# Banded attention and a feed-forward layer in one kernel: the order of its work planned anew, output rooms and the read of a flag moved

## The chip, the cores and the metric

The kernel runs on one core of one Trainium2 chip. The metric is the device time of one execution in microseconds (us); for several runs it is their median. The engines of the core are TensorE (PE, with its weight loads as PEld), VectorE (DVE), ScalarE (ACT), GpSimd (POOL) and SyncE (SP), which here only issues DMAs. Each takes its own instructions strictly in order.

## What is computed

Attention over a band of 96 keys and 8 global keys with a distance bias, for 4 batches of 8 heads, 768 positions and 64 channels, and then a feed-forward layer with a leaky step on the 3072 x 512 result:

```python
scores = scale * np.matmul(q, k.transpose(0, 1, 3, 2))
...
bias = -slopes[:, None, None] * dist[None, :, :]
scores = np.where(keep, scores + bias[None, :, :, :], -1000000000.0)
a = np.exp(scores - np.max(scores, axis=-1, keepdims=True))
a = a / (np.sum(a, axis=-1, keepdims=True) + 1e-09)
x = np.matmul(a, v)          # then to (3072, 512)
...
h = x @ w_in                 # (512, 2048)
g = np.maximum(0.01 * h, h)
return (g @ w_out).astype(np.float32)
```

## The kernel before

All of the fast path is one list of words, `ORDER`, written out in the file by a planner. `fast_path` reads it word by word, and each word issues a few instructions, pinned to that order on their engines. A word is a letter for the kind of work, a number for the unit or turn, and perhaps a part. An engine runs its own instructions in the order in which their words stand, and waits where data or a room is not ready; so what stands ahead of an instruction on its own engine can hold it up.

**Attention** has 48 units of 4 heads x 128 queries. Lq, Lk, Lv load the operands (SP). S makes the scores (PE, into `ps_av`), B adds the bias and takes the maximum (DVE, in four parts .0 to .3, L333), E the exponential (ACT, L349), N the reciprocal of the sum and M the quotients (DVE). From unit 16 on D turns 32 x 32 blocks (DVE, L391) and writes the result to memory (SP, L360), and I fetches it back in four DMAs (SP, L366): I must wait in SP's queue until the write has landed. V multiplies with the values (PE, L470) into the free columns of a `ps_av` tile that also holds the scores of a later unit; Xh copies the result out (ACT, L480).

**The feed-forward layer** starts with chunks 0 to 2 of the rows, in words F (first product, PE), g (gates, on ACT and DVE in turns), H (second product, PE) and P (outputs). The weights come as 64-bit floats in pieces: Lw loads one (SP, L227), c converts it in four parts on ACT and DVE. The rooms of `load_piece` are four. Each product is made of three: the operands are split into a high part, rounded to a shorter format, and the rest. O stores the converted second weights to memory (SP, L708), R brings them back (POOL's DMA queue, L711).

**Chunks 3 to 6** take two blocks of weight columns at a time, in turns Q, y, d, r, h, l, J. A group of 8 turns serves one chunk of 512 rows: turns 0 to 7, 8 to 15, 16 to 23, 24 to 31. The first product is made in seven half-size products Q p.1 to Q p.7 of combined weights and operands instead of eight. C (16 parts: 12 passes on POOL, L664, and 4 roundings on ACT, L667) builds the combined weights of a turn once, during the turns before; A (POOL, L717), Y (ACT) and z (POOL or DVE) combine the operands of a chunk. The y word copies the first product out of its PSUM tile (ACT, L731), and Q p.2, which writes the same columns, waits for it. The words d add up the seven products (DVE, L737), r is the leaky step (DVE, L741), h the rounding (ACT, L744), l the rest (DVE, L747). J p.ij are the second products (PE, L755), issued a turn later among the Q of turn p + 1. At a chunk's end U copies four accumulators out (`late`; ACT L763, or DVE L761 with a `v`) and sends each to the output (SP, L765): U3 to U6, each with parts 0 to 3. The room `ob` of a part is `at((14, 20)[tt % 2], [DM])`: two rooms in turns. So parts 2 and 3 wait until the DMAs of parts 0 and 1 have landed.

**The flag.** The fast path is right for short bands only. Behind it `band_holds` tests the counts and the maxima (small DVE passes, L885 to L891), turns the column of 128 results with a product (PE, L894), reduces it (L895), casts it (L896), and `values_load` brings it into a register of each engine (L1086). A branch on it (L1088) skips a general path behind it, and the program's end follows (L1142).

**Planner's leads before.** From unit 16 on S of a unit n + 2 stands with V of unit n, in the same `ps_av` tile (`bank(n + 2)`).

Of the kernel before, what the change touches and what calls it, by code (L numbers as in the profile page):

```python
# [11 lines left out]
F32 = mybir.dt.float32  # L12
# [7 lines left out]
P = 128  # L20
# [38 lines left out]
P22.1 Lv17 P22.2 Xh14 Xl14 T15 g24a S16 g24b K15 k15 H23 Lk19 B16.0 g24c B16.1 E16.0 B16.2 B16.3 E16.1 g24d E16.2 V15
E16.3 N16 F25 M16.0 Lv18 Xh15 M16.1 M16.2 Xl15 M16.3 D16 S17 g25a H24 g25b I16 B17.0 g25c B17.1 E17.0 B17.2 Lq10 B17.3  # L60
E17.1 g25d F26 E17.2 Lk20 E17.3 N17 M17.0 M17.1 M17.2 V16 M17.3 g26a D17 S18 Lv19 Xh16 g26b H25 B18.0 g26c B18.1 E18.0
B18.2 I17 B18.3 E18.1 g26d E18.2 F27 Lk21 E18.3 N18 M18.0 M18.1 M18.2 M18.3 H26 D18 g27a g27b g27c I18 V17 g27d S19
Xh17 Lv20 F28 Lq11 B19.0 B19.1 E19.0 B19.2 Lk22 B19.3 E19.1 E19.2 E19.3 H27 g28a N19 M19.0 M19.1 M19.2 M19.3 D19 F29
g28b g28c I19 g28d V18 g29a g29b S20 Lv21 Xh18 Y3.0 H28 Lk23 B20.0 g29c B20.1 B20.2 E20.0 B20.3 E20.1 g29d E20.2 z3.0
F30 E20.3 N20 M20.0 M20.1 M20.2 M20.3 H29 D20 g30a g30b g30c V19 I20 g30d S21 Xh19 Lv22 F31 Lq12 B21.0 B21.1 E21.0
B21.2 Lk24 B21.3 E21.1 E21.2 E21.3 H30 g31a N21 M21.0 M21.1 M21.2 M21.3 D21 F32 g31b V20 g31c I21 g32a g31d S22 Xh20
g32b Lv23 H31 B22.0 B22.1 Lk25 E22.0 B22.2 B22.3 E22.1 E22.2 E22.3 F33 P31.0 g32c g32d P31.1 V21 g33a P31.2 H32 Xh21
g33b Lv24 N22 g33c M22.0 F34 M22.1 g33d M22.2 M22.3 D22 H33 g34a g34b F35 g34c I22 g34d H34 g35a g35b g35c F36 g35d
H35 g36a g36b g36c F37 g36d H36 g37a g37b g37c S23 g37d F38 Lq13 B23.0 B23.1 E23.0 B23.2 Lk26 B23.3 E23.1 H37 E23.2
g38a E23.3 g38b F39 N23 g38c C0.0 M23.0 g38d C0.1 M23.1 H38 M23.2 g39a M23.3 C0.2 D23 C0.4 C0.3 F40 g39b C0.5 g39c I23  # L70
g39d C0.6 V22 g40a C0.8 C0.7 g40b S24 Lv25 Xh22 C0.10 H39 g40c Lk27 B24.0 B24.1 C0.9 g40d A3.1 E24.0 B24.2 E24.1 B24.3
F41 E24.2 C0.11 E24.3 Y3.4 N24 C0.12 H40 M24.0 g41a M24.1 M24.2 C0.14 g41b C0.13 M24.3 g41c F42 D24 C0.15 C1.0 g41d
V23 z3.4 C1.1 g42a I24 g42b H41 C1.2 Xh23 g42c A3.2 Lv26 C1.3 g42d S25 F43 Lq14 B25.0 A3.3 Y3.5 B25.1 B25.2 Lk28 B25.3
E25.0 z3.5 E25.1 H42 A3.4 g43a E25.2 g43b E25.3 F44 C1.4 g43c N25 Y3.1 g43d C1.5 M25.0 Y3.6 M25.1 H43 M25.2 C1.6 M25.3
g44a D25 C1.8 C1.7 V24 g44b C1.10 C1.9 S26 g44c C1.11 I25 Xh24 F45 g44d B26.0 C1.12 B26.1 E26.0 Lv27 B26.2 C1.14 B26.3
E26.1 H44 Lk29 g45a z3.1p E26.2 g45b E26.3 F46 g45c N26 C1.13 z3.6p g45d M26.0 H45 M26.1 g46a M26.2 M26.3 C1.15 g46b
D26 g46c F47 C2.0 g46d C2.1 H46 C2.2 g47a I26 Y3.2 g47b C2.4 C2.3 z3.2 Q0.1 g47c C2.8 Y3.3 Q0.6 g47d C2.5 y0.1 z3.3
H47 C2.9 C2.6 d0a C2.11 C2.7 Q0.2 P47.0 C2.10 Q0.5 d0b C2.12 V25 d0c Q0.3 C2.14 C2.13 Lv28 Xh25 S27 C2.15 d0d r0.0
# [24 lines left out]
d9a E35.3 J8.01 d9b Q9.5 N35 M35.0 M35.1 J8.02 M35.2 d9c Q9.3 M35.3 D35 J8.03 d9d Q9.7 R10.0 r9.0 J8.10 I35 d9e h9.0
J8.11 d9f l9.0 Q9.4 J8.12 d9g J8.13 r9.1 V34 h9.1 R10.1 S36 l9.1 Lv37 Xh34 Q10.1 B36.0 B36.1 E36.0 J9.00 B36.2 B36.3
y10.1 Q10.6 E36.1 Lk39 E36.2 Q10.2 E36.3 d10a N36 J9.01 d10b Q10.5 M36.0 M36.1 M36.2 M36.3 J9.02 D36 Q10.3 d10c J9.03
d10d Q10.7 r10.0 I36 R11.0 J9.10 h10.0 d10e J9.11 d10f l10.0 Q10.4 J9.12 d10g J9.13 r10.1 V35 h10.1 R11.1 S37 l10.1
Lv38 Xh35 Q11.1 Lq20 B37.0 B37.1 E37.0 J10.00 B37.2 Lk40 B37.3 y11.1 Q11.6 E37.1 E37.2 Q11.2 E37.3 d11a N37 J10.01
d11b Q11.5 M37.0 M37.1 M37.2 M37.3 J10.02 D37 Q11.3 d11c J10.03 d11d Q11.7 r11.0 I37 R12.0 J10.10 h11.0 d11e J10.11
# [53 lines left out]
def fast_path(ctx, tc, qp, kp, vp, wi, wo, nvec, weights, woboth, nmall, out, B, H, S):  # L162
# [380 lines left out]
    def step(word):  # L543
# [602 lines left out]
```

## Time and profile before

| | us |
|---|---|
| median of 3 runs | 682.49 (681.49 to 683.00) |
| the profiled execution | 680.44 |
| its span, first to last instruction | 678.6 |
| outside its span | 1.84 |
| mean granted clock of TensorE | 0.978 |
| PE busy | 629.2 (93%) |
| DVE busy | 486.6 (72%) |
| ACT busy | 279.8 (41%) |
| POOL busy | 204.3 (30%) |

The busy shares are means over stages that differ: which engine others wait for is read from the stretch. A window's granted clock is a mean too: 1.00 is 2.4 GHz throughout, 0.50 is 1.2 GHz throughout.

### The profile page before, as it was taken

How to read it: one execution, taken by the hardware profiler on the slowest of the kernel's cores; microseconds unless marked ns; L12 is line 12 of the kernel's file. 1: busy time of each engine (PE TensorE's matmuls, PEld its weight loads, DVE VectorE, ACT ScalarE, POOL GpSimd, SP SyncE). 2: the span in 40 equal slices, each digit the busy share in tenths (PEclk: the TensorE clock that was granted, in tenths of full speed). 3: DMA queues.
4: the chain of work that ended last, by engine and by line, in shares of the span. 5: the costliest groups of instructions: out<-in, count | busy, mean ns of one | idle time of the engine just before them, and what ended most of it. 6: DMA issues, size and time to landing. Idle time of an engine off the chain costs nothing. (4 is left out here: it accounts for less than half of the span.)

```text
span 678.6 us, 16087 instructions
## 1 busy us (share of the span) xinstructions
PE 629.2 (93%) x6187; PEld 540.9 (80%) x6187; DVE 486.6 (72%) x1277; ACT 279.8 (41%) x802; POOL 204.3 (30%) x267
## 2 busy tenths in 40 slices
PE   5599999999999998889899799999989999999993
PEld 4478888898888867778688688888778888989982
DVE  6899998875666597988578566778757767555551
ACT  4877766546453455524225232324332223211111
POOL 3433401004100289887636001116100115211100
PEclk9879999999999999999899989999989999999998
DMA  8766744696666233446485865665775653533421
GB/s 282 255 202 193 224 136 141 213 397 209 189 182 211 82 115 125 136 128 188 142 248 150 240 195 171 205 194 177 206 224 164 197 145 88 160 94 94 125 63 68
DMA packets 71334, 118.07 MB, mean 174 GB/s; under 512 B 8784, under 2 KB 27216, under 8 KB 71248
## 3 DMA queue, kind: packets, MB, share of 16 engines
q1 hardware_dynamic: 54928, 85.48, 39.3%
q0 software_dynamic: 16320, 31.46, 16.6%
q8 instruction: 51, 0.84, 0.5%
q14 instruction: 35, 0.29, 0.1%
HBM read 90.18 MB, written 26.74 MB: 172 GB/s over the span
## 5 line engine op out<-in xcount | busy, mean ns | idle before, releaser
L744 ACT CAST rounded<-room 128x512 fp32r<-128x512 f32 x64 | 39.7, 620 | 199.2 <-DVE room L741 155.2
L711 POOL DMA_DIRECT2D wo<-w x60 | 43.5, 726 | 234.5 <-PE ps_two L755 232.3
L755 PE MATMUL ps_o<-wo,rounded 128*128 128x512 f32 x320 | 96.6, 400 | 0.0
L755 PE MATMUL ps_two<-wo,rounded 128*128 128x512 f32 x320 | 95.5, 396 | 0.0
L349 ACT ACTIVATE pr<-pr,nmall 128x192 f32<-128x192 f32 (+1 forms) x192 | 83.8, 440 | 19.8 <-DVE nmall L333 19.2
L737 DVE TENSOR_TENSOR room<-ps_o,room 128x256 f32<-128x256 f32 x128 | 53.9, 421 | 34.3 <-PE ps_o L700 23.2
L1029 PE MATMUL ps_h<-rounded,wih 128*128 128x384 f32 (+1 forms) x192 | 63.1, 329 | 0.5 <-ACT atz L1041 0.5
L737 DVE TENSOR_TENSOR room<-ps_q,room 128x256 f32<-128x256 f32 x96 | 39.9, 416 | 32.6 <-PE ps_q L700 31.5
L700 PE MATMUL ps_q<-rounded,wih 128*128 128x256 f32 x256 | 50.0, 289 | 12.5 <-ACT room L731 12.5
L1030 PE MATMUL ps_h<-rounded,wih 128*128 128x384 f32 (+1 forms) x192 | 61.2, 319 | 0.0
L1031 PE MATMUL ps_h<-rounded,wil 128*128 128x384 f32 (+1 forms) x192 | 61.1, 318 | 0.0
L755 PEld LDWEIGHTS ps_o<-wo,rounded 128*128 128x128 f32 x320 | 54.9, 192 | 5.9
L755 PEld LDWEIGHTS ps_two<-wo,rounded 128*128 128x128 f32 x320 | 54.3, 189 | 5.9
L700 PEld LDWEIGHTS ps_o<-rounded,wo 128*128 128x128 f32 x384 | 53.9, 188 | 6.3 <-DVE room L737 0.7
L700 PE MATMUL ps_o<-rounded,wo 128*128 128x256 f32 x384 | 56.3, 282 | 0.0
L700 PEld LDWEIGHTS ps_q<-rounded,wih 128*128 128x128 f32 x256 | 42.6, 194 | 16.4 <-ACT room L731 13.5
L333 DVE CUSTOM_DVE_ANT_0 pr<-ps_av,nbw 128x192 f32<-128x192 f32 x140 | 41.8, 352 | 16.0 <-ACT room L480 13.2
L741 DVE SCALAR_TENSOR_TENSOR room<-room 128x512 f32<-128x512 f32 x64 | 48.2, 754 | 2.2
L1043 DVE SCALAR_TENSOR_TENSOR atz<-atz 128x384 f32<-128x384 f32 (+1 forms) x48 | 29.7, 618 | 19.5 <-ACT atz L1041 19.4
L470 PEld LDWEIGHTS ps_av<-room,vr 64*64 64x64 f32 x1472 | 31.0, 134 | 15.1 <-PE ps_two L755 7.8
L386 DVE TENSOR_SCALAR pr<-pr,rs 128x192 f32<-128x192 f32 (+1 forms) x128 | 41.2, 371 | 0.7
L1029 PEld LDWEIGHTS ps_h<-rounded,wih 128*128 128x128 f32 x192 | 36.3, 189 | 5.6 <-issue 2.8
(136 smaller groups left out, 1439.0 us busy)
## 6 DMA issues: line engine op xcount, KB each, us to landing
wo<-w POOLq DMA_DIRECT2D x60, 512.0 KB, 4.2
via<-pr SPq DMA_DIRECT2D x28, 384.0 KB, 2.4
room<-via SPq DMA_DIRECT2D x112, 96.0 KB, 2.6
kr<-in_kp_dram SPq DMA_DIRECT2D x40, 256.0 KB, 3.9
vr<-in_vp_dram SPq DMA_DIRECT2D x40, 256.0 KB, 3.2
room<-in_wo_dram SPq DMA_DIRECT2D x16, 512.0 KB, 4.5
room<-in_wi_dram SPq DMA_DIRECT2D x16, 512.0 KB, 4.7
w<-wo SPq DMA_DIRECT2D x16, 512.0 KB, 7.0
```

The source lines that it names most:

```text
L333: pin(nc.vector.tensor_tensor_reduce(out=head(u, pr, a, j), in0=own(u, ps[:, j, a * KW:(a + 1) * KW]), in1=nb, scale=-0.125, scalar=3.0e38 ...
L349: pin(nc.scalar.activation(out=p, in_=p, func=AF.Exp, scale=-1.0, bias=nm[:, 2 * a + j:2 * a + j + 1], accum_out=sm[:, 2 * a + j:2 * a + j ...
L386: pin(nc.vector.tensor_scalar(out=p, in0=p, scalar1=rs[:, n:n + 1], scalar2=1.0, op0=ALU.mult, op1=ALU.mult))
L700: tc.keep_in_program_order(nc.tensor.matmul(out, lhsT=lhs[:, k], rhs=rhs[:, k], start=k == 0 and m == 0, stop=k == 1 and m == 2))
L711: pin(nc.gpsimd.dma_start(out=wboth[:, :, f % 4], in_=w2[f].rearrange("x p d -> p x d")))
L737: pin(nc.vector.tensor_tensor(out=quarter[i][o], in0=lps[b][:, h * HB:(h + 1) * HB], in1=quarter[a][q], op=ALU.add))
L741: pin(nc.vector.scalar_tensor_tensor(out=t, in0=t, scalar=0.01, in1=t, op0=ALU.mult, op1=ALU.max))
L744: pin(nc.scalar.copy(out=lg(i)[0], in_=lt[i]))
L755: tc.keep_in_program_order(nc.tensor.matmul(o, lhsT=lhs, rhs=rhs, start=f == 0 and m == 0, stop=f == NF - 1 and m == 2))
L1029: tc.keep_in_program_order(nc.tensor.matmul(ps, lhsT=wih[:, k, fs], rhs=xh[:, k, :CT], start=(k == 0), stop=False))
L1030: tc.keep_in_program_order(nc.tensor.matmul(ps, lhsT=wih[:, k, fs], rhs=xl[:, k, :CT], start=False, stop=False))
L1031: tc.keep_in_program_order(nc.tensor.matmul(ps, lhsT=wil[:, k, fs], rhs=xh[:, k, :CT], start=False, stop=(k == NK - 1)))
```

## The change

- `ORDER` is written anew from its 459th word on. Words before that stand as they did. No word goes but U6.1, which becomes U6.1v (DVE in place of ACT); X0 to X3 are new.
- From unit 16 on S of unit n + 3, no longer n + 2, stands with V of unit n (`bank(n + 3)`).
- Output rooms: U5 has four (14, 20, 22, 25) and U6 four (0, 2, 4, 6); U3 and U4 keep two.
- The flag: the small passes become X0 (`band_part`, pinned within turn 20), and a one-column product of the results with themselves counts those that hold (X1, PE, in turn 25). X2 compares the count (DVE), X3 loads the register on all engines, between J30.13 and J31.00. `band_holds` goes.

The diff, its core (from `ORDER` the lines in which words of the prediction stand; units and turns keep their numbers):

```diff
@@ ORDER, from the 459th word
-g16d c27a c26d H16 c27b g17a c28a g17b F18 Lw30 c27c c28b g17c O0 T14 g17d g18a O1 c28c g18b H17 c28d g18c Lw31 g18d
...
-J3.11 C7.6 d4f l4.0 Q4.4 C7.8 C7.7 J3.12 C7.10 d4g C7.9 J3.13 r4.1 C7.11 V29 h4.1 C7.12 S31 l4.1 C7.14 Lv32 Xh29 C7.13
-Q5.1 R4.1 Lq17 B31.0 B31.1 E31.0 J4.00 B31.2 Lk34 B31.3 y5.1 Q5.6 C7.15 E31.1 E31.2 Q5.2 R5.0 d5a E31.3 J4.01 N31 d5b
...
-M34.2 M34.3 D34 J7.03 Q8.7 d8d R9.0 r8.0 J7.10 I34 d8e J7.11 h8.0 d8f U3.0 Q8.4 l8.0 U3.1 J7.12 d8g J7.13 r8.1 V33
-h8.1 R9.1 S35 l8.1 Lv36 Xh33 Q9.1 B35.0 U3.2 B35.1 J8.00 B35.2 y9.1 B35.3 Lq19 U3.3v Q9.6 E35.0 Lk38 E35.1 Q9.2 E35.2
...
-h16.1 R17.1 S43 l16.1 Lv44 Xh41 Q17.1 B43.0 U4.2 B43.1 J16.00 B43.2 y17.1 B43.3 U4.3v Lq23 Q17.6 E43.0 E43.1 Lk46
...
-J31.03 J31.10 J31.11 U6.0 J31.12 U6.1 J31.13 U6.2 U6.3v
...
+F21 g20d O9 O10 H20 g21a Lw31 g21b g21c O11 F22 g21d O12 c31a H21 O13 g22a c31b Xh12 Xl12 O14 V13 g22b c31c Lq8 g22c
...
+J3.12 C6.15 d4g J3.13 C7.0 r4.1 V29 R5.1 h4.1 S32 Lv32 C7.1 Xh29 l4.1 Q5.1 I31 C7.2 B32.0 J4.00 B32.1 y5.1 C7.4 B32.2
...
+d5g C7.15 J4.13 r5.1 V30 l5.0 h5.1 R6.1 S33 l5.1 Lv33 Xh30 A4.1 Q6.1 B33.0 B33.1 J5.00 E33.0 B33.2 y6.1 B33.3 I32 Q6.6
...
+M35.2 Q8.7 M35.3 R9.0 d8d J7.10 r8.0 J7.11 d8e U3.0 d8f Q8.4 h8.0 D34 J7.12 U3.1 d8g J7.13 l8.0 V33 R9.1 r8.1 S36 I34
+Xh33 D35 Q9.1 h8.1 J8.00 l8.1 y9.1 U3.2 Lv36 Q9.6 B36.0 Lk39 B36.1 E36.0 Q9.2 B36.2 E36.1 d9a J8.01 E36.2 B36.3 d9b
+E36.3 Q9.5 U3.3v J8.02 N36 I35 Q9.3 d9c M36.0 J8.03 M36.1 d9d Q9.7 r9.0 R10.0 J8.10 d9e h9.0 J8.11 d9f l9.0 Q9.4 M36.2
...
+M43.3 Lv44 Xh41 l16.1 Q17.1 B44.0 J16.00 B44.1 E44.0 B44.2 y17.1 Lk47 Q17.6 B44.3 U4.2 D43 Q17.2 E44.1 E44.2 J16.01
...
+Q25.4 J24.12 d25g J24.13 r25.1 X1 h25.1 R26.1 Q26.1 X2 l25.1 J25.00 y26.1 Q26.6 Q26.2 d26a J25.01 d26b Q26.5 J25.02
...
+r31.1 X3 h31.1 J31.00 l31.1 J31.01 J31.02 J31.03 J31.10 J31.11 U6.0 J31.12 U6.1v J31.13 U6.2 U6.3v
...
-            banks[n, 1] = ps_lead.tile([P, 2, 512], F32, tag="ps_ov", name="ps_ov") if n < BANKS - 1 else bank(n + 2)
+            banks[n, 1] = ps_lead.tile([P, 2, 512], F32, tag="ps_ov", name="ps_ov") if n < BANKS - 1 else bank(n + (2 if n < BY_DVE else 3))
...
-            ob = at((14, 20)[tt % 2], [DM])
+            ob = at(((14, 20, 14, 20), (14, 20, 22, 25), (0, 2, 4, 6))[max(n - 4, 0)][tt], [DM])
...
+        elif what == "X":
+            yet = (lambda: band_part(nc, pin, nvec, nmall, fl),
+                   lambda: tc.keep_in_program_order(nc.tensor.matmul(held[0:1, 0, 0:1], lhsT=fl[:, 0:1], rhs=fl[:, 0:1],
+                                                                     start=True, stop=True)),
+                   lambda: pin(nc.vector.tensor_scalar(out=flag, in0=held[0:1, 0, 0:1], scalar1=P - 0.5, scalar2=None,
+                                                       op0=ALU.is_ge)),
+                   lambda: read.append(nc.values_load(flag, min_val=0, max_val=1,
+                                                      skip_runtime_bounds_check_because="the flag is a comparison")))
...
+    return read[0]
...
-        with tc.tile_pool(name="fin", bufs=1) as fin:
-            flag = nc.values_load(band_holds(tc, fin, nvec, nmall), min_val=0, max_val=1,
-                                  skip_runtime_bounds_check_because="the flag is a product of comparisons")
+        flag = fast_path(tc, a["qp"], a["kp"], a["vp"], a["wi"], a["wo"], nvec, weights, woboth, nmall, out, B, H, S)
         with tc.If(flag == 0):
```

## Rows read from the trace of the kernel before

**Rows 1.** Windows: length, busy of PE, PEld, DVE, ACT, POOL; PEclk, DMA share, GB/s

```profile
0.00:40.00 40.00, 23.84 (x556) 19.95 (x557) 31.96 (x120) 26.44 (x89) 16.55 (x36) 0.88 0.77 252
...
235.00:303.00 68.00, 60.38 (x578) 49.31 (x572) 58.03 (x127) 31.13 (x98) 58.80 (x69) 1.00 0.42 125
303.00:329.00 26.00, 25.37 (x277) 21.67 (x268) 19.88 (x50) 9.56 (x32) 19.84 (x27) 1.00 0.56 167
329.00:341.00 12.00, 8.89 (x55) 7.72 (x48) 7.70 (x24) 4.04 (x14) 7.73 (x10) 0.86 0.40 124
...
384.00:396.00 12.00, 7.56 (x35) 6.64 (x34) 4.90 (x19) 2.84 (x11) 0.00 (x0) 0.72 0.74 219
396.00:488.00 92.00, 91.85 (x895) 78.84 (x894) 70.22 (x195) 32.05 (x95) 21.65 (x23) 1.00 0.64 191
488.00:500.00 12.00, 7.29 (x42) 6.50 (x39) 4.66 (x19) 2.99 (x11) 0.00 (x0) 0.86 0.77 239
```

**Rows 2.** Waits of PE, whole span: us in total, times, longest

```profile
PE ps_q L700 <- ACT room L731: 12.5, 4, 4.7
...
PE ps_o L700 <- DVE room L737: 4.3, 3, 2.3
```

**Rows 3.** Timeline of ACT, 378 to 394: start, us, instruction, idle before

```profile
380.08 1.07 ACT L763 COPY room<-ps_o 128x512 f32<-128x512 f32 x2
...
389.58 0.58 ACT L763 COPY room<-ps_two 128x512 f32<-128x512 f32 x1 [5.36 <-DMA out_dram<-room]
390.06 0.38 ACT L731 COPY room<-ps_q 128x256 f32<-128x256 f32 x1
```

**Rows 4.** Timeline of SP's queue, 360 to 394

```profile
378.61 0.56 SPq L360 DMA_DIRECT2D via<-pr  x1
383.36 1.87 SPq L366 DMA_DIRECT2D room<-via  x4
385.33 0.94 SPq L765 DMA_DIRECT2D out_dram<-room  x2
```

**Rows 5.** Timeline of ACT, 322 to 338

```profile
333.61 0.41 ACT L667 CAST wo<-room 128x256 fp32r<-128x256 f32 x1 [1.33 <-POOL room L664]
...
334.37 0.35 ACT L731 COPY room<-ps_q 128x256 f32<-128x256 f32 x1
```

**Rows 6.** What line L667 (ACT) waits for, whole span: us, times

```profile
  POOL room L664: 18.5, 10
```

**Rows 7.** Groups of DVE, 235 to 303: count, busy us, mean ns, idle before

```profile
L741 DVE SCALAR_TENSOR_TENSOR room<-room 128x512 f32<-128x512 f32 x6 | 5.6, 933 | 0.2
```

**Rows 8.** Groups of DVE, 400 to 412

```profile
L741 DVE SCALAR_TENSOR_TENSOR room<-room 128x512 f32<-128x512 f32 x2 | 1.4, 692 | 0.1
```

**Rows 9.** Line L765 (outputs U): time from issue to landing

```profile
DMA to landing us min/median/max: 2.0/2.9/4.3
```

**Rows 10.** Timeline of SP's queue, 125 to 170

```profile
142.43 1.30 SPq L284 DMA_DIRECT2D qs<-in_qp_dram  x1
```

**Rows 11.** Line L708 (stores O): time from issue to landing

```profile
DMA to landing us min/median/max: 5.9/7.0/8.3
```

**Rows 12.** Timeline of PE, 150 to 166: the first product of H22

```profile
157.73 0.39 PE L1065 MATMUL ps_o<-wo,rounded 128*128 128x512 f32 x1
```

**Rows 13.** Timeline of all engines, 655 to 680

```profile
666.75 0.40 PE L755 MATMUL ps_two<-wo,btz 128*128 128x512 f32 x1
...
668.51 0.69 DVE L761 COPY room<-ps_two 128x512 f32<-128x512 f32 x1 [5.69 <-DMA out_dram<-room]
...
669.25 0.27 PE L894 MATMUL row<-ident,fl 128*1 128x128 f32 x1 [2.11 <-DVE room L761]
```

**Rows 14.** Line L1086 (load of the flag's register): duration in ns, start

```profile
L1086 PEldq TENSOR_LOAD <-flag x1: 647/647/647, 670.2 to 670.2; - x1
```

**Rows 15.** Line L1088 (branch on the flag): duration in ns, start

```profile
L1088 SPq COMPARE_BRANCH  x1: 45/45/45, 670.9 to 670.9; - x1
```

**Rows 16.** Line L1142 (end of the program): durations in ns, first and last start

```profile
L1142 SPq EVENT_SEMAPHORE  x14: 17/28/28, 677.0 to 678.6; - x14
```

More of the change, by code (lines that the diff above doesn't have):

```diff
@@ L59 @@
[L59 to L78, printed above, removed]
@@ L104 @@
[L104 to L108, printed above, removed]
@@ L149 @@
-h29.0 d29e J28.11 d29f l29.0 Q29.4 J28.12 d29g J28.13 r29.1 Q30.1 h29.1 R30.1 J29.00 y30.1 l29.1 Q30.6 Q30.2 d30a
-J29.01 d30b Q30.5 J29.02 d30c Q30.3 J29.03 d30d Q30.7 r30.0 R31.0 J29.10 h30.0 d30e J29.11 d30f l30.0 Q30.4 J29.12
-d30g J29.13 r30.1 Q31.1 h30.1 R31.1 J30.00 y31.1 l30.1 Q31.6 Q31.2 d31a J30.01 d31b Q31.5 J30.02 d31c Q31.3 J30.03
-d31d Q31.7 r31.0 J30.10 h31.0 d31e J30.11 d31f l31.0 Q31.4 J30.12 d31g J30.13 r31.1 J31.00 h31.1 J31.01 l31.1 J31.02
-J31.03 J31.10 J31.11 U6.0 J31.12 U6.1 J31.13 U6.2 U6.3v
+g16d c27a c26d H16 c27b g17a c28a g17b F18 Lw30 c27c c28b g17c O0 T14 g17d g18a O1 c28c g18b H17 c28d g18c Lk16 g18d
@@ new lines @@
+l15.0 h15.1 S43 Lv43 R16.1 Xh40 M42.0 Q16.1 l15.1 Lk46 J15.00 M42.1 y16.1 M42.2 Q16.6 M42.3 B43.0 Q16.2 Lq23 B43.1
+E43.0 d16a J15.01 E43.1 d16b Q16.5 B43.2 B43.3 E43.2 J15.02 D42 E43.3 Q16.3 d16c J15.03 N43 d16d I42 Q16.7 R17.0 r16.0
+J15.10 d16e h16.0 J15.11 d16f U4.0 l16.0 Q16.4 U4.1 M43.0 J15.12 d16g J15.13 r16.1 V41 M43.1 R17.1 h16.1 M43.2 S44
+M43.3 Lv44 Xh41 l16.1 Q17.1 B44.0 J16.00 B44.1 E44.0 B44.2 y17.1 Lk47 Q17.6 B44.3 U4.2 D43 Q17.2 E44.1 E44.2 J16.01
+d17a E44.3 d17b Q17.5 U4.3v I43 J16.02 N44 Q17.3 d17c M44.0 J16.03 M44.1 d17d Q17.7 R18.0 r17.0 J16.10 d17e h17.0
@@ L154 @@
+d30e J29.11 d30f l30.0 Q30.4 J29.12 d30g J29.13 r30.1 Q31.1 h30.1 R31.1 J30.00 y31.1 l30.1 Q31.6 Q31.2 d31a J30.01
+d31b Q31.5 J30.02 d31c Q31.3 J30.03 d31d Q31.7 r31.0 J30.10 h31.0 d31e J30.11 d31f l31.0 Q31.4 J30.12 d31g J30.13
+r31.1 X3 h31.1 J31.00 l31.1 J31.01 J31.02 J31.03 J31.10 J31.11 U6.0 J31.12 U6.1v J31.13 U6.2 U6.3v
 """
@@ L704, in late @@
     def late(what, n, part):
-        nonlocal ps_h, ps_o
+        nonlocal ps_h, ps_o, held
         p = n % (NF // 2)
@@ L765, in late @@
             pin(nc.sync.dma_start(out=out[r0:r0 + P, :], in_=ob))
+        elif what == "X":
[6 more added lines that the diff above has]
+                                                      skip_runtime_bounds_check_because="the flag is a comparison")))
+            if n == 1:
+                held = ps_x.tile([P, 2, 512], F32, tag="ps_av", name="ps_fl")
+            yet[n]()
         else:
             raise ValueError(what)
-    lps = []
-    ps_h = ps_o = None
+    lps, read = [], []
+    held = ps_h = ps_o = None
+    fl = arena.tile([P, 4], F32, name="fl")
+    flag = arena.tile([1, 1], I32, name="flag")
     for word in ORDER.split():
         step(word)
+    return read[0]
 def split_float64(tc, pin, w, raw, dh, dl):
@@ L875, in read_counts, with band_part @@
     return nvec
[L878 to L897 removed]
+def band_part(nc, pin, nvec, nmall, fl):
+    pin(nc.vector.tensor_reduce(out=fl[:, 3:4], in_=nmall, axis=mybir.AxisListType.X, op=ALU.max))
+    pin(nc.vector.tensor_scalar(out=fl[:, 0:1], in0=nvec[:, 0:1], scalar1=float(G), scalar2=None, op0=ALU.is_le))
+    pin(nc.vector.tensor_scalar(out=fl[:, 1:2], in0=nvec[:, 1:2], scalar1=1.0, scalar2=None, op0=ALU.is_ge))
+    pin(nc.vector.tensor_scalar(out=fl[:, 2:3], in0=nvec[:, 1:2], scalar1=float(WIN + 1), scalar2=None, op0=ALU.is_le))
+    pin(nc.vector.tensor_scalar(out=fl[:, 3:4], in0=fl[:, 3:4], scalar1=9.0e8, scalar2=None, op0=ALU.is_lt))
+    pin(nc.vector.tensor_tensor(out=fl[:, 0:2], in0=fl[:, 0:2], in1=fl[:, 2:4], op=ALU.mult))
+    pin(nc.vector.tensor_tensor(out=fl[:, 0:1], in0=fl[:, 0:1], in1=fl[:, 1:2], op=ALU.mult))
 def general_attention(tc, qt, kt, vt, nvec, xs, B, H, S):
```

166 lines of the change are left out of this document (83 added, 83 removed).

## The prediction

> **What bounds the kernel now.** I began with the windows view, cut so that each stretch holds one kind of behaviour [rows 1]. In 396 to 488 TensorE (PE) is busy 91.85 of 92 us at the full granted clock, so over most of the span the kernel is bound by the length of PE's own queue, which the change does not shorten. Time can be won only where PE stands idle or runs below its full clock. The windows show five such places. From 0 to 40 PE is busy 23.84 us. From 235 to 303 it is busy 60.38 of 68, from 303 to 329 25.37 of 26. The three 12 us windows from 329, 384 and 488 are busy 8.89, 7.56 and 7.29, each with a granted clock under 1. The last place is the tail, after the last product.
>
> The view of waits says who is late [rows 2]: in the steady part PE waits 12.5 us in 4 waits (longest 4.7) for the y copy of ACT (L731), and 4.3 us for the sums of DVE (L737). I then read ACT's and SP's timelines around the longest waits. In the second turn after an output, ACT stands 5.36 us for an output DMA before it copies U3.2, and y9.1, for which PE waits, stands behind that copy in ACT's queue [rows 3]. Why the DMA is late is in SP's queue [rows 4]: the fetch I34 (L366) cannot start before the data that L360 began to write at 378.61 has landed, it goes out at 383.36, and the two outputs U3.0 and U3.1 (L765), whose copies were long done, wait behind it until 385.33. A room of the two is therefore given back late. The window from 488 repeats this with U4.
>
> The window from 329 has another cause [rows 5]: y5.1 stands behind a rounding of the weight combination (L667) that waits 1.33 us for POOL, and behind an exponential. That is no single case: L667 waits 18.5 us for POOL in 10 waits [rows 6]. Between 235 and 303 POOL is busy 58.80 and DVE 58.03 of 68 us [rows 1], and DVE's passes are longer there: L741 takes 933 ns on the mean [rows 7] and 692 in 400 to 412 [rows 8]. Three in-order queues that are nearly full, with ACT's waiting for POOL's, bound that stretch.
>
> **The prices.** An idle window costs its idle time and what PE loses at the lower of its two clock levels (1.2 GHz, half of the full 2.4). From 384: 12 less 7.56 is 4.44 idle; a mean clock of 0.72 is 0.28 x 12 = 3.4 lost. Where both overlap it counts once, so 6.1 to 7.8; I take 7.0. From 488: 4.71 + 0.14 x 12 = 6.4. From 329: 3.11 + 1.7 = 4.8. Together 18.2 us. The stretches 235 to 303 and 303 to 329 hold 7.62 + 0.63 = 8.25 us of idle time.
>
> **The change, part by part.** The first 458 words of the order are the same, so the head and its 16 us of idle time stay.
>
> *The outputs U3 and U4.* Their rooms are the same two as before. What moves is the order. U3.0 now stands ahead of D34 and I34 in SP's queue, so its DMA goes out when ACT's copy is done, near 380.7, and lands 2.0 to 4.3 us later [rows 9], before 385; U3.1's is behind D34's write alone. In ACT's queue y9.1 now precedes U3.2. So even a late DMA no longer stops PE. What is late next there is U3.2 itself, which the third accumulator of the next turn (J8.02) waits for; it stands three products further on. For U4 the same holds, with one exponential, E44.0, still ahead of y17.1. I leave 0.5 us for each of the two windows: 13.4 - 1.0 = 12.4 gained, bounds 0 and 13.4.
>
> *The combinations C0 to C7 (12 passes on POOL, 4 roundings on ACT each).* Same instructions, spread wider: C0 begins at the same place, but C7.15, which stood behind Q5.6, now stands behind J4.12, three quarters of a turn later (a turn has 15 words Q and J). Eight turns' worth of C takes most of a turn more, so POOL's passes are some tenth thinner, and no C rounding stands between h4.1 and y5.1 any more. C7 is first needed by Q7.6, still over a turn away. I take the window from 329 as won but for 0.5 (4.3 gained). Of the 8.25 idle us before it I take 5, by the nearest rows: the stretch before has DVE at 85%, and a tenth less POOL work in it lets DVE's passes shrink toward 692 ns, but not all the way. Bounds: 0, and all 8.25.
>
> *Scores three units ahead of their outputs.* S and B of a unit move one turn earlier against its V. Per turn this adds nothing: one unit enters and one leaves. It costs that the transposing passes and quotients now stand among DVE's sums. In 396 to 488 DVE is busy 70.22 of 92 [rows 1], so a pass finds a gap of its size; cost 0, and without the cover one pass of about 0.69 a turn [rows 8]. What is queued behind each is the next sum, and PE's next product waits for that.
>
> *The late weight piece.* Lw31 goes behind eight of the stores O in SP's queue, about to where Lq8 went out at 142.43 [rows 10]. The stores there land 5.9 to 8.3 us after issue [rows 11], so the piece is there by 150.7; its five passes over 128x512 at 0.7 end near 154.3. H22 needs it, at 157.73 before [rows 12]. Cover 3.4 us, cost 0; beyond that, ACT and DVE, with the gates of F22 behind these passes, and so PE, pay one for one.
>
> *The tail.* Before, the last product ends at 666.75 + 0.40 = 667.15. DVE's last copy waits for an output room until 668.51; then PE turns the flag at 669.25, and DVE reduces and casts it [rows 13], all engines load it [rows 14], SP branches at 670.9 [rows 15], and its clean-up ends at 678.6 [rows 16]: 7.7 us after its branch. After: four rooms, so U6.3v runs right behind the product, to 667.9; SP issues its DMA until 668.25 and branches. The same 7.7 us follow, which makes 676.0, or 2.6 less. The flag costs elsewhere: PE loads the register between J30.13 and J31.00, 0.65 [rows 14], and turns the flag in the order, at most 0.27 [rows 13] with a gap: 0.3. DVE's and ACT's loads lie beside products. Net 1.6 gained, bounds 1.0 and 2.6.
>
> The Trainium skill prices that load otherwise: "Runtime: NRT & Kernel Launch", in its breakdown of the preamble and postamble, gives TENSOR_LOAD about 1.3 us. By that the net would be 1.0, an estimate; the trace's load of one register took 0.65.
>
> The sum: 680.44 - 12.4 - 4.3 - 5.0 - 1.6 = 657.1 for an execution like the profiled one. The median of the runs lies 2.05 above that one; so 659.2.
>
> **Rivals.** (a) *The combination stretch stays full.* The passes of POOL and DVE lengthen each other wherever they meet (933 against 692), and thinning POOL by a tenth only moves the meetings. Then neither the 5 nor the 4.3 come: 668.5. For it: DVE at 85% there. Against: the waits named are on single late instructions. The Trainium skill says the same of the mechanism ("SBUF — State Buffer", on who interferes with whom: a VectorE instruction with two SBUF inputs and a GpSimd one that reads SBUF exclude each other for the whole instruction). L741 reads its tile twice and shows the longer time; whether whole instructions exclude each other no row here tells.
>
> (b) *All idle time of these places goes*: 680.44 - 18.2 - 8.25 - 1.6 = 652.4, so 654.4. For it: 396 to 488 shows that such turns can run without a gap.
>
> (c) *The output waits only move.* U3 and U4 still have two rooms. If SP is held by another fetch as it was by I34, the copies wait as before, and E36.0 and the next y with them: 657.1 + 12.4, so 671.6.
>
> (d) *Slower: DVE's queue becomes the bound of the steady turns.* In the 18 turns with attention work a transposing pass or a quotient now stands ahead of the sums and leaky steps; if their gap is not there, each turn loses up to two passes, 1.38 [rows 8], or 24.8 in all: 684. It decides from 1.3 a turn. Against it: DVE idles a quarter of that stretch.
>
> (e) *The flag read isn't ahead.* If the load still comes last, only the rooms help, and the gain of the tail is gone: 660.8.
>
> **How the numbers follow.** Forecast 659.2: 0.49. (a) 0.17, (b) 0.17, (c) 0.06, (d) 0.07, (e) 0.04. The range from 651 to 670 holds the forecast, (a), (b) and (e) with their spread, and leaves out (c), (d) and the far ends. A measurement of this kernel tells about 0.2% from no change, 1.4 us. Only (d) reaches there: 0.05 slower, 0.02 within it; faster 0.93.
>
> **What would show it.** Right: no ACT wait for an output DMA of over 1 us before a y; PE's waits for L731 under 3 us; a granted clock of 1.00 from 45 on to the end of the products; waits of L667 for POOL well under 18.5; the load of the flag before the last products, and SP's branch about 1 us after the last of them. Wrong: DVE over 90% in turns without POOL work, PE waiting for L737 or L747 turn after turn (d); 235 to 329 still 8 us idle (a); H22 waiting for a rounding of the last piece.

## The result, and the profile after

The changed kernel takes 662.52 us (median of 4 runs, 661.06 to 664.36) against 682.10 (4 runs, 681.49 to 683.00): a ratio of 0.9713, interval 0.9686 to 0.9741. Its profiled execution took 662.32 with a span of 660.5. The forecast was 659.2, the range 651 to 670.

The sum came near by parts that err in opposite directions. To place them I measured the same thing in each trace. A step is the time from the start of one word's products to the start of the next word's; what it lasts beyond the tenth percentile of its kind (the same kind of word) I count as PE time lost. The count depends on how kinds are told apart: with all attention words taken as one kind, the differences between two traces in the stretches from 235 on come out up to about 1 us different. So its tenths carry no weight. Summed by stretch, in us:

| stretch | before | after |
|---|---|---|
| 0 to 45 | 23.0 | 22.8 |
| 45 to 235 | 8.5 | 8.1 |
| 235 to 361, where C builds the combined weights | 21.7 | 21.8 |
| 361 to the last product | 24.9 | 11.4 |
| last product to the end of the span | 11.5 | 7.0 |

The outputs gave 13.5, the tail 4.4 (by the spans and the ends of the last products), and the combination stretch, from which the forecast took 9.3, nothing.

Windows of after (length, busy of PE, PEld, DVE, ACT, POOL, PEclk, DMA share, GB/s), cut as in [rows 1]:

```profile
235.00:303.00 68.00, 63.03 (x567) 51.96 (x567) 59.78 (x130) 31.62 (x97) 53.95 (x64) 1.00 0.45 141
303.00:329.00 26.00, 22.65 (x220) 18.87 (x222) 20.58 (x52) 8.93 (x29) 20.89 (x26) 1.00 0.57 169
329.00:341.00 12.00, 11.62 (x93) 9.44 (x83) 9.01 (x25) 4.56 (x15) 9.73 (x13) 1.00 0.63 180
341.00:353.00 12.00, 10.24 (x101) 8.49 (x100) 6.43 (x21) 3.84 (x13) 4.87 (x6) 0.86 0.70 182
384.00:396.00 12.00, 12.00 (x125) 10.50 (x124) 9.77 (x31) 4.34 (x14) 1.43 (x2) 1.00 0.97 272
396.00:488.00 92.00, 91.60 (x850) 78.98 (x850) 71.88 (x202) 34.08 (x104) 20.11 (x22) 1.00 0.74 211
488.00:500.00 12.00, 12.00 (x123) 10.37 (x122) 9.35 (x29) 3.63 (x12) 1.24 (x3) 1.00 0.78 210
```

The windows from 384 and 488 are full and at the full clock, as forecast. The one from 329 is nearly full too, and 235 to 303 is 4.97 us idle where it was 7.62. But stops have come elsewhere: 303 to 329 is 3.35 us idle where it was 0.63, and 341 to 353 is 1.76 idle with a clock of 0.86. From 235 to 329 PE stands 8.32 us in all, before 8.25: the sign that the prediction had named for rival (a).

What ACT waits for in 235 to 361 of after (us in total, times, longest), and under it the same view for POOL:

```profile
ACT wo L667 <- DMA wo<-w: 32.6, 9, 5.5
...
ACT wih L667 <- POOL room L664: 5.6, 4, 3.4
ACT wo L667 <- POOL room L664: 3.1, 5, 0.7
```

```profile
POOL wo L664 <- DMA wo<-w: 9.6, 4, 2.7
```

Here is another wait. The rounding L667 waits 8.7 us for POOL in this stretch, before 18.5; and it waits 32.6 us for the DMA `wo<-w`, which is R: the second layer's weights on their way back. The last of these waits shows how it works. Timelines of POOL, of ACT and of PE, of after, from 340:

```profile
340.49 0.74 POOL L711 DMA_DIRECT2D wo<-w  x1 [0.41 <-POOL wo L664]
341.25 1.20 POOL L664 TENSOR_TENSOR room<-room 128x256 f32<-128x256 f32 x1
344.50 1.42 POOL L664 TENSOR_TENSOR wo<-room,wo 128x256 fp32r<-128x256 f32 x2 [2.05 <-DMA wo<-w]
```

```profile
344.51 0.41 ACT L667 CAST wo<-room 128x256 fp32r<-128x256 f32 x1 [5.51 <-DMA wo<-w]
344.82 1.13 ACT L744 CAST rounded<-room 128x512 fp32r<-128x512 f32 x2
```

```profile
345.49 0.73 PE L755 MATMUL ps_o<-wo,rounded 128*128 128x512 f32 x2 [1.47 <-ACT rounded L744]
```

R goes out at 340.49 and lands 4.0 us later; a rounding on ACT and a low pass on POOL (it computes the rest of a combined weight) start in the same instant. Two roundings h (L744) of the running turn stand behind it on ACT, and PE waits 1.47 us for them. Yet R and C share no byte. R fills columns f of both halves of `wboth` (high and low parts) in one DMA; the high parts of the combined weights lie behind the fourth such block of the high half, so between the two places that R writes. The dependency is kept for the stretch from the first to the last byte, and these results of C lie inside it. (The run with R in two, below, shows this: there the waits are gone.)

The view puts a wait down to what came last, and not all of the 32.6 us are R's. In the row above the rounding had been waiting for POOL's pass of 341.25, which ended at 342.45; R held it for the last 2.06 of its 5.51 us. Set against the end of the pass that each rounding needs, R's own part in the nine waits is 17.0 us. The rest is POOL being late, as before.

### The profile page after: what moved, and what is told of

Read it like the earlier page. It is cut to its first block, busy times and chain, and to the rows that moved or that the text cites. A ratio compares the mean times of both kernels' runs of the same rounds, so it can differ in the third digit from the quotient of the medians.

```text
span 660.5 us, 16106 instructions
## 1 busy us (share of the span) xinstructions
PE 624.2 (95%) x6188; PEld 535.2 (81%) x6188; DVE 488.3 (74%) x1277; ACT 280.1 (42%) x801; POOL 203.0 (31%) x265
## 5 line engine op out<-in xcount | busy, mean ns | idle before, releaser
L744 ACT CAST rounded<-room 128x512 fp32r<-128x512 f32 x64 | 39.5, 620 | 171.4 <-DVE room L741 168.4
L737 DVE TENSOR_TENSOR room<-ps_o,room 128x256 f32<-128x256 f32 x128 | 53.8, 421 | 34.8 <-PE ps_o L700 26.7
L737 DVE TENSOR_TENSOR room<-ps_q,room 128x256 f32<-128x256 f32 x96 | 40.3, 420 | 32.8 <-PE ps_q L700 31.4
L755 PEld LDWEIGHTS ps_two<-wo,rounded 128*128 128x128 f32 x320 | 54.1, 188 | 6.1
L333 DVE CUSTOM_DVE_ANT_0 pr<-ps_av,nbw 128x192 f32<-128x192 f32 x140 | 42.2, 352 | 13.6 <-ACT room L480 7.7
L741 DVE SCALAR_TENSOR_TENSOR room<-room 128x512 f32<-128x512 f32 x64 | 50.7, 793 | 1.9
L386 DVE TENSOR_SCALAR pr<-pr,rs 128x192 f32<-128x192 f32 (+1 forms) x128 | 45.2, 395 | 0.7
L1046 DVE SCALAR_TENSOR_TENSOR atz<-atz 128x384 f32<-128x384 f32 (+1 forms) x48 | 27.2, 567 | 20.8 <-ACT atz L1044 20.7
L470 PEld LDWEIGHTS ps_av<-room,vr 64*64 64x64 f32 x1472 | 30.5, 134 | 13.2 <-PE ps_two L755 7.1
```

The lines of the kernel that those rows point to most:

```text
L333: pin(nc.vector.tensor_tensor_reduce(out=head(u, pr, a, j), in0=own(u, ps[:, j, a * KW:(a + 1) * KW]), in1=nb, scale=-0.125, scalar=3.0e38 ...
L386: pin(nc.vector.tensor_scalar(out=p, in0=p, scalar1=rs[:, n:n + 1], scalar2=1.0, op0=ALU.mult, op1=ALU.mult))
L737: pin(nc.vector.tensor_tensor(out=quarter[i][o], in0=lps[b][:, h * HB:(h + 1) * HB], in1=quarter[a][q], op=ALU.add))
L741: pin(nc.vector.scalar_tensor_tensor(out=t, in0=t, scalar=0.01, in1=t, op0=ALU.mult, op1=ALU.max))
L744: pin(nc.scalar.copy(out=lg(i)[0], in_=lt[i]))
L755: tc.keep_in_program_order(nc.tensor.matmul(o, lhsT=lhs, rhs=rhs, start=f == 0 and m == 0, stop=f == NF - 1 and m == 2))
```

## The experiments

Where a kernel has R in two DMAs, the lines behind 711 are numbered 4 higher (L741 is L745), and with the fills 9 higher (L750).

### The outputs: which queue makes the stop

The order of U3 and U4 alone, in the kernel before (fragments of the order):

```diff
-J7.10 I34 d8e J7.11 h8.0 d8f U3.0 Q8.4 l8.0 U3.1 J7.12
+J7.10 d8e J7.11 h8.0 d8f U3.0 Q8.4 l8.0 U3.1 I34 J7.12
...
-B35.0 U3.2 B35.1 J8.00 B35.2 y9.1 B35.3
+B35.0 B35.1 J8.00 B35.2 y9.1 U3.2 B35.3
...
-J15.10 I42 d16e J15.11 h16.0 d16f U4.0 Q16.4 l16.0 U4.1 J15.12
+J15.10 d16e J15.11 h16.0 d16f U4.0 Q16.4 l16.0 U4.1 I42 J15.12
...
-B43.0 U4.2 B43.1 J16.00 B43.2 y17.1 B43.3
+B43.0 B43.1 J16.00 B43.2 y17.1 U4.2 B43.3
```

> The kernel before, with four moves of words: I34 behind U3.1, U3.2 behind y9.1, I42 behind U4.1, U4.2 behind y17.1. Nothing else changes, the rooms are the same two. Theory (the order alone makes the two stops): the windows from 384 and 488 are busy 12 of 12 at a granted clock of 1.00, and the span falls by 12 to 13.5 us. Rival (the waits only move, since two rooms stay): ACT or DVE still waits over 3 us for an output DMA in each, and the span falls by 4 us at most.

Measured: 668.34, ratio 0.9824 (0.9785 to 0.9862), 13.2 us below the kernel before of its chip (681.58); PE's loss behind 361 fell from 24.9 to 11.5, and PE is busy 12.00 of 12 us in both windows, at a clock of 1.00. All of the gain of the outputs is in these moves.

They are two moves at each place, one in SP's queue (I behind the outputs) and one in ACT's (U3.2 behind y). The next kernel takes the first of the four hunks above and the last (the fetch behind two outputs, not three as the expectation has it):

> The kernel before with half of the outputs' edit at each place: at U3 only the fetch I34 is moved behind the three outputs (SP's queue), at U4 only the output U4.2 is moved behind y17.1 (ACT's queue). If each stop has the cause that the prediction gave it (at 384 the transfer from ACT's queue ahead of y, at 488 the same or the fetch that stands at its room on SP), the half that touches the cause frees its stop and the other leaves it. By the trace, ACT stood 5.36 us at its output transfer and the fetch stood 4.7 us on SP with the outputs behind it: moving the fetch alone should free the stop at 384 (7 us), because the output that ACT's transfer waits for then leaves early; moving the transfer alone should free the one at 488 (6 us). Then 668 to 670. If only ACT's place matters, 675 to 676 with the stop at 384 left; if only SP's matters, the same with the stop at 488 left.

Measured: 674.90 (2 runs), ratio 0.9898 (0.9876 to 0.9920). The stop at 384 went; the one at 488 stayed, 4.1 us. Its mirror takes the other two hunks:

> The kernel before with the other halves: at U3 only the output U3.2 is moved behind y9.1 (ACT's queue), at U4 only the fetch I42 is moved behind the first two outputs (SP's queue). By the run of the first halves it is SP's queue at both places (there the stop at 384 went with the fetch and the one at 488 stayed without it): then here the stop at 488 goes and the one at 384 stays, 675 to 676, and ACT still stands 4 to 5 us at U3.2, now behind y9.1, with the next scores behind it. If ACT's place ahead of y frees a stop by itself as the prediction had it, both go: 668 to 670.

Measured: 674.80, ratio 0.9914 (0.9872 to 0.9955). The stop at 488 went, the one at 384 stayed. SP's queue it is, at both places. With the fetch still ahead, ACT's place behind y buys little: PE stands 4.1 us at U4, before 4.7. SP's queue and ACT's timeline of the first halves, at U4:

```profile
483.23 1.75 SPq L366 DMA_DIRECT2D room<-via  x4
485.08 2.12 SPq L765 DMA_DIRECT2D out_dram<-room  x2
```

```profile
483.91 0.37 ACT L731 COPY room<-ps_q 128x256 f32<-128x256 f32 x1 [0.51 <-PE ps_q L700]
489.00 0.58 ACT L763 COPY room<-ps_two 128x512 f32<-128x512 f32 x1 [4.72 <-DMA out_dram<-room]
```

The y copy is in time now (483.91), and U4.2 waits alone. But the stop only changes its way. The mirror's waits, 376 to 400:

```profile
DVE room L761 <- ACT room L763: 4.5, 1, 4.5
ACT room L763 <- DMA out_dram<-room: 4.2, 1, 4.2
...
PE ps_o L700 <- DVE room L737: 3.6, 1, 3.6
```

DVE's copy U3.3v waits until ACT's U3.2 has run, the sums d of the next products stand behind U3.3v on DVE, and PE waits for a sum instead of for y.

### The tail

The flag ahead and U6's four rooms, in the kernel before (X0 in turn 20, X1 and X2 in 25, X3 ahead of J31.00):

```diff
-            ob = at((14, 20)[tt % 2], [DM])
+            ob = at(((14, 20, 14, 20), (0, 2, 4, 6))[n == 6][tt], [DM])
...
-J31.03 J31.10 J31.11 U6.0 J31.12 U6.1 J31.13 U6.2 U6.3v
+J31.03 J31.10 J31.11 U6.0 J31.12 U6.1v J31.13 U6.2 U6.3v
```

> The kernel before with the changed tail alone: flag worked out in turns 21 to 26 and loaded between r31.1 and J31.00, U6 with four rooms, U6.1 on DVE; the order is otherwise that of before, U5 keeps two rooms. By the prediction's steps: 7.7 us from SP's branch to the end, 0.65 us of PE for the register, 1.6 us gained. By the trace of the changed kernel (5.1 us from branch to end, no time of PE for the register): 4.0 to 4.5 us gained.

Measured: 678.05 (10 runs), ratio 0.9951 (0.9934 to 0.9968), 3.5 below the kernel before of its chip, 2.2 to 4.5 by the interval. That is neither of the two amounts expected. In its trace (the longest of the ten executions) the last product to SP's branch takes 1.8 us, before 3.75; the branch to the end 7.2, before 7.7: 2.4 in all. The 5.1 from branch to end of the kernel after did not come with its flag code.

### The combination stretch: R in two

The kernel after, with R in two DMAs, one for each half, whose stretches no longer cover C's results:

```diff
+            if n < 9:
+                for x in range(2):
+                    pin(nc.gpsimd.dma_start(out=wboth[:, x, f % 4], in_=w2[f, x]))
+            else:
                 pin(nc.gpsimd.dma_start(out=wboth[:, :, f % 4], in_=w2[f].rearrange("x p d -> p x d")))
```

> The changed kernel; of the words R0 to R8 each fetch of two stored weight halves is made of two DMAs, one for each half, so that the stretch of memory between the halves, where the combined weights lie, is no longer part of one write. POOL issues some 12 more DMAs of 0.74 us. Theory (the roundings L667 wait for the landing of R, 32.6 us in 9 waits, and hold up h, y and E behind them): these waits go, PE's lost time from 235 to 361 falls from 22 us to under 14, the kernel is 5 to 10 us faster than the changed one, 653 to 658. Rival (POOL and DVE are simply full there and lengthen each other): not faster than the changed one, and up to 3 us slower for the added DMAs.

Measured: 657.53 (656.05 to 658.19), ratio 0.9662 (0.9628 to 0.9696). Against after that is 5.0 us by the medians (the ranges of the two do not meet), 0.0051 or 3.5 us by the ratios, each to the kernel before of its own chip. All waits of L667 and L664 for the DMA are gone, and PE's loss in 235 to 361 fell from 21.8 to 16.8, not below 14. So the wait for R is real and is worth 3.5 to 5; something else holds the rest. This version beats both kernels.

What is left of ACT's waits says what after had hidden. The same view as above, of this run:

```profile
ACT wo L667 <- POOL room L664: 15.3, 12, 3.3
...
ACT wih L667 <- POOL room L664: 3.1, 2, 2.0
```

L667 waits 18.4 us for POOL, as much as in the kernel before (18.5). So the new order had not taken these waits away: in after, 15.6 us of waiting for POOL (32.6 less 17.0) stood under R's name, because R came last.

The same edit in the kernel before:

> The kernel before with only R0 to R8 split in two. In its trace ACT's roundings waited 1.3 us once for a landing of the second layer's weights, against 32.6 us in 9 places after. If that wait is new with the changed order, the split gives the kernel before nothing: 680 to 683, within 0.3% of it. If the split is worth its 5 us whatever the order, 677.

Measured: 677.45 (5 runs, 673.75 to 680.46), ratio 0.9915 (0.9889 to 0.9940). The medians differ by 4.8. My theory fell: the wait was not new. I had looked only at what ACT waits for. POOL's timeline of before:

```profile
320.02 0.74 POOL L711 DMA_DIRECT2D wo<-w  x1 [0.77 <-POOL wo L664]
324.07 1.09 POOL L664 TENSOR_TENSOR wo<-room,wo 128x256 fp32r<-128x256 f32 x1 [3.31 <-DMA wo<-w]
```

POOL stood 3.31 us for R's landing just ahead of the stop at 329. The rounding that waited for POOL [rows 5] was late because POOL had been. With R in two, L667 waits 10.0 us for POOL in place of 18.5, and the window is full:

```profile
329.00:341.00 12.00, 12.00 (x119) 10.05 (x118) 9.90 (x27) 4.61 (x15) 8.92 (x13) 1.00 0.87 259
```

This trace is of the longest of the five executions, 680.46, as long as the profiled one of before: it lost the time again in other places, 303 to 329 (2.04 us idle, before 0.63) and the two stops at the outputs. That the edit shortens the kernel is read from the five times, not from this trace.

Last, whether an order alone could avoid it: the kernel after with C0 to C7 begun earlier (C0.0 behind H35 in place of B24.2, C7.15 behind J3.12 in place of J4.12), R as one DMA, and `t3` of the first two of them in another room:

```diff
-        t1, t2, t3 = (at(o, [2, P]) for o in (14, 15, 20))
+        t1, t2, t3 = (at(o, [2, P]) for o in (14, 15, 13 if p < 2 else 20))
```

> The kernel after with the first eight combinations begun 10 to 17 us earlier, and each R as one DMA as in the kernel after. If it is the order of R and C alone that makes them meet (C's writes of the combined weights while an R is under way), the earlier C has most of its writes done before R4 is issued, the waits of ACT and POOL for R fall from 42 us to under 15, and the time is within 1.5 us of the early order with the split, 654 to 657. If the R's have to be split for it, the waits stay at 25 us or more and it stays 4 to 6 us above, 658 to 662.

Measured: 661.54, ratio 0.9710 (0.9684 to 0.9736), the same as after. ACT and POOL still wait 36.2 us for R (27.2 and 9.0). R comes with every turn, and so does C; some meet in either order. With R in two (the next run) the same order is 0.0112 of the ratio faster, 7.6 us: while R is one DMA, beginning C earlier gives nothing.

### The combination stretch: what else holds it

The same early order with R in two:

> The kernel after with R0 to R8 split in two, and the first eight combinations (C0 to C7) begun 10 to 17 us earlier in the order; the third temporary of the first two of them lies in another room, because in the kernel after POOL stood 45 us (170 to 217) at room 20 until an output's DMA had left it. If the 17 us that PE still loses between 235 and 361 are POOL and DVE being full (the queue of C's passes), the same passes begun in POOL's empty time take that to 10 to 12 us, and the kernel comes 4 to 7 us below the split alone: 651 to 654. If DVE's slower passes beside POOL are the cause, they only move with POOL's work to an earlier stretch and the gain is under 1 us, 656 to 658.

Measured: 654.71 (653.96 to 656.79), ratio 0.9598 (0.9579 to 0.9617): the fastest version whose results are whole. Against R in two alone that is 4.4 us by the ratios (0.0064) and 2.8 by the medians, and PE's loss in 235 to 361 fell only from 16.8 to 15.0. (The profiled execution is the longest of the four.) C's last pass on POOL began at 326.5, with R in two alone at 338.7. So both theories had a part: C came earlier, but POOL's empty time was not used, since it stood 54.1 us, 51.7 of them in one wait, at low parts that wait for ACT's roundings at their place in the order. (In after, POOL stood 42.8 us at C0's first pass into room 20, from 172.6 on, not 45 as the expectation has it.)

Then C's work itself, by a size. The kernel after, with C's passes and roundings on 16 of their 128 columns, so that the combined weights are only begun:

```diff
+            out, a, b = (x[:, :, :16] for x in (out, a, b))
...
-            pin(nc.scalar.copy(out=out, in_=a))
+            pin(nc.scalar.copy(out=out[:, :, :16], in_=a[:, :, :16]))
```

> The changed kernel with the combination of weights cut down: each pass and rounding of C works on 16 of its 128 columns, so the combined weights are not those of the reference. POOL's passes of 0.75 to 0.85 us become short; every word, wait and DMA stays. Rival (fullness): DVE's L741 is back near 0.69 us, PE's lost time from 235 to 361 falls from 22 us to under 9, 12 us or more gained. Theory (waits for the landing of R): L667 still waits over 20 us for DMAs, PE's lost time there stays over 15 us, 3 to 6 us gained.

Measured: 646.25 (2 runs), ratio 0.9493 (0.9451 to 0.9535). The loss in 235 to 361 is 6.25. The waits for R went too; why, this run does not show. So it tells the whole price of C beside the turns, 15.6 us by PE's loss, and not its parts. R in two tells 5.0 of them.

The rest could be POOL's own fullness, or what its reads do to DVE. In the kernel with R in two, I put constant fills, which read nothing, in the place of the passes that write temporaries (eight of the twelve in each combination, not seven as the expectation has it):

```diff
+            if out is t1 or out is t2 or out is t3:
+                pin(eng.memset(out, 0.0))
+                pin(eng.memset(out, 0.0))
+                pin(eng.memset(out[:, 0], 0.0))
+            else:
+                pin(eng.tensor_tensor(out=out, in0=a, in1=b, op=op))
```

> The kernel after with R0 to R8 split in two, and the seven passes of each combination that write its temporaries replaced by constant fills of the same length of time on POOL (two of 128x256 and one of 128x128, about 0.86 us in all), which read nothing; the combined weights are therefore not those of the reference. POOL is as busy and everything waits for it in the same order. If POOL's own fullness sets the loss between 235 and 361, PE still loses 15 to 18 us there and the time stays at 655 to 659. If it is DVE's evictions, stretched by POOL's reads of the memory, DVE's pass of line 741 comes back from 0.84 to about 0.75 us and PE's loss falls to 6 to 10 us, 647 to 651.

Measured: 654.18 (2 runs), ratio 0.9594 (0.9563 to 0.9625), between the two. POOL is as busy (103.01 us of 235 to 361, against 102.06), DVE's busy time falls from 114.46 to 98.53, and PE's loss from 16.8 to 13.2. The leaky step (L741 in after) lasts 0.84 us on the mean in 235 to 361; in after it is 0.82, with R in two 1.22, with the short passes 0.79. (So the 0.84 that the expectation starts from is not that of the kernel it changes.) About 3.6 us are then DVE's waiting for POOL's reads, and four passes in twelve still read. How the other 6.9, down to the 6.25 of the short passes, are shared between that and a full POOL these runs do not tell. The largest stop left with the fills has both in its chain (timelines of ACT, DVE and PE):

```profile
332.47 0.41 ACT L672 CAST wo<-room 128x256 fp32r<-128x256 f32 x1 [3.17 <-POOL room L667]
```

```profile
334.31 2.44 DVE L756 TENSOR_TENSOR btz<-room,rounded 128x512 fp32r<-128x512 f32 x1
```

```profile
337.92 0.68 PE L705 MATMUL ps_q<-rounded,wih 128*128 128x256 f32 x2 [2.27 <-ACT room L740]
```

A rounding of C waits 3.17 us for POOL, and the roundings h and the rests l behind it come late. The second rest then lasts 2.44 us: it ends 0.56 after a pass of POOL (an A, 334.89 to 336.19) that reads the room. B, E and y come behind it, and PE stands 2.27 us.

How DVE is held shows best with R in two, where POOL has fewer gaps. Timelines of DVE, then of POOL:

```profile
307.83 3.40 DVE L745 SCALAR_TENSOR_TENSOR room<-room 128x512 f32<-128x512 f32 x1
...
311.61 1.72 DVE L745 SCALAR_TENSOR_TENSOR room<-room 128x512 f32<-128x512 f32 x1
```

```profile
307.86 0.76 POOL L664 TENSOR_TENSOR room<-room 128x256 f32<-128x256 f32 x1
308.56 1.43 POOL L664 TENSOR_TENSOR wo<-room,wo 128x256 fp32r<-128x256 f32 x2
309.95 0.73 POOL L664 TENSOR_TENSOR room<-wih,wil 128x256 f32<-128x256 f32 x1
310.91 1.10 POOL L713 DMA_DIRECT2D wo<-w  x2 [0.22 <-issue]
312.01 0.76 POOL L664 TENSOR_TENSOR room<-wih,wil 128x256 f32<-128x256 f32 x1
312.85 1.06 POOL L664 TENSOR_TENSOR room<-room 128x256 f32<-128x256 f32 x1
```

The leaky step (L741, here L745), 0.69 us in the stretch where POOL is less busy [rows 8], stands through four passes of POOL without a gap, and ends 0.55 after the last of them, at 311.23. The next one ends 0.56 after POOL's pass at 312.01, and the POOL pass that follows is 0.3 longer than its 0.75. PE's timeline has the price:

```profile
314.52 0.50 PE L759 MATMUL ps_o<-wo,rounded 128*128 128x512 f32 x1 [1.16 <-DVE rounded L751]
```

The third product of J3.00 waits 1.16 us for the pass that follows the two. With fills in POOL's queue (timelines of DVE and POOL):

```profile
271.14 0.68 DVE L750 SCALAR_TENSOR_TENSOR room<-room 128x512 f32<-128x512 f32 x1
```

```profile
271.10 0.31 POOL L665 MEMSET room<- 128x256 f32 x1
271.47 0.31 POOL L666 MEMSET room<- 128x256 f32 x1
```

This step is not lengthened. The sums L737, which read one operand from PSUM and one from the room, take 0.41 to 0.42 us on the mean in every one of these runs.

## Why the forecast came near, and where it was wrong

**The outputs**: the size was right (12.4 forecast, 13.5 in after, 13.2 alone), and SP's queue was the cause [rows 4]. The step that gave ACT's move a share in it, "So even a late DMA no longer stops PE", was wrong. With y ahead and the DMA late, PE still lost 4 us, by way of DVE's U3.3v (3.6 at U3, and 4.1 at U4 by the same way). In after it is SP's order that lets the DMA go in time: its first two outputs leave ahead of the fetch (SP's queue).

```profile
379.81 0.34 SPq L765 DMA_DIRECT2D out_dram<-room  x1
...
380.82 0.35 SPq L765 DMA_DIRECT2D out_dram<-room  x1
384.15 1.74 SPq L366 DMA_DIRECT2D room<-via  x4
```

**The combination stretch** is the step that failed: 4.3 for the window from 329 and 5.0 for the idle time ahead of it, of which nothing came. The prediction traced the late y5.1 to POOL [rows 5, 6] and stopped there. One step further back stood R's DMA. Thinning C over more of the order put C's results among more of the R's: 42.2 us of waits of ACT and POOL for the DMA in after, 8.0 before. And it did not shorten POOL's own lateness, which the step took for granted: L667 waits 18.5 us for POOL before, 8.8 in after where R hides part of it, and 18.4 in the same order once R is in two. So the sign that I had named for this step, "waits of L667 for POOL well under 18.5", came true without the gain, and meant nothing. Nor did DVE's passes shrink toward 692 ns, as the step had it: L741 takes 816 ns on the mean of 235 to 361, before 839. Rival (a) was right that nothing would come there. Its mechanism, POOL and DVE lengthening each other, is part of it: of the 15.6 us that C costs in after, about 5 are R's and about 3.6 that mechanism's; the rest these runs do not divide.

On that mechanism the prediction left open whether whole instructions exclude each other. The trace above shows that they do: the step waits out four passes, not a share of them. The Trainium skill ("SBUF — State Buffer", section "Who interferes with whom") calls the port pair that VectorE and GpSimd share an exclusive lock, and says that a VectorE instruction with two SBUF inputs contends with a GpSimd one that reads SBUF, not with one that only writes it. The row of 3.40 beside passes and that of 0.68 beside fills agree with both halves of it. That the loser blocks for the whole instruction the section spells out only for VectorE's two-port modes; here the row of 3.40 is what shows it.

**The tail** was sized at 1.6 and measured at 4.4. PE's load of the register, priced at 0.65, cost nothing. Line L772 (the load) of after, and PE's timeline around J31.00, which stands behind it in the order:

```profile
L772 PEldq TENSOR_LOAD <-flag x1: 490/490/490, 644.2 to 644.2; - x1
```

```profile
647.48 0.39 PE L755 MATMUL ps_two<-wo,btz 128*128 128x512 f32 x1
647.71 1.56 PE L755 MATMUL ps_o<-wo,rounded 128*128 128x512 f32 x6
```

The load ran 3.5 us ahead of the product, while products issued before it were still at work, and left no gap. The gain ahead of the branch, 2.6 gross in the prediction, was 1.8, since U6.3v does not run right behind the product: DVE's timeline of after has it behind ACT's copy.

```profile
654.18 0.69 DVE L761 COPY room<-ps_two 128x512 f32<-128x512 f32 x1 [1.31 <-ACT room L763]
```

The other 2.6 come from a term that I had held fixed at 7.7: from SP's branch at 655.4 to the end at 660.5 it is 5.1 in after. Why stays open: it was 7.2 with the same flag code in the order of before, 5.1 to 5.6 in five kernels made from after, and 7.7 to 8.4 in four made from before with its flag as it was. So the term was no constant even there.

```profile
L1088 SPq COMPARE_BRANCH  x1: 45/45/45, 655.4 to 655.4; - x1
```

**The step from the profiled execution to the median**, 2.05, was 0.2 in after.

**What was costed at nothing** cost nothing. The scores three units ahead leave 396 to 488 with PE busy for 91.60 of 92 us and DVE for 71.88, so rival (d) has no place. PE's loss in 45 to 235, where the late weight piece is, went from 8.5 to 8.1.

**The other signs.** PE's waits for L731 are 2.8 us, under 3 as forecast. The clock of 1.00 up to the end of the products did not come (0.86 in 341 to 353), and SP's branch comes 1.9 us behind the last product, not about 1.

**The sum, put right**: 680.44, less 13.5 and 4.4, less 0.6 ahead of 235, plus 0.1 for the combination stretch, is 662.0; the profiled execution took 662.32. The forecast for it was 657.1: 9.4 too much in one place, and 1.1, 2.8 and 0.6 too little in three others. That the median came within 3.3 us of the forecast is luck as far as these errors cancel.

## What to carry to other kernels

When a late instruction waits for another engine, ask what that engine itself last waited for, and go on until the first wait in the chain: moving the work in between moves the wait along with it. A view of waits names what came last; another that was late too shows only when the first is gone. A DMA that writes two far places in one call can hold everything that lies between them; two calls cost POOL 0.36 us more here (1.10 for 0.74) and gave 3.5 to 5. And where an in-order queue carries both a wait-prone fetch and the DMA that gives a room back, the order of those two decides, more than the order on the engines that fill the room.

## What the runs showed of the hardware

- A register load that stands between two products in the order of PE ran 3.5 us before the second of them and took nothing from PE (0.49 us, L772).
- A DVE pass with two operands in SBUF was held by four POOL passes in a row with no gap between them, 3.40 us for 0.69; a POOL fill beside such a pass did not hold it (0.68), and nor was a DVE sum with one operand from PSUM lengthened (0.41 to 0.42 in every run).
- From the last branch to the end of the program SP took 5.1 to 8.4 us with the same instructions to run at the end.
